# Score visits in pairs, with two score tiles and a third bank for the first matmul

## The chip, the cores and the metric

The kernel runs on one core of one Trainium2 chip. The metric is the device time of one execution in microseconds (us). The five engines of the core are TensorE (PE), VectorE (DVE), ScalarE (ACT), GpSimd (POOL) and SyncE (SP, which only issues DMAs here). PE writes its results into PSUM, which has eight banks of 512 fp32 columns on 128 partitions.

## The reference

Attention with a sliding window of 128 keys and a linear distance bias, in fp32, for 8 batches, 8 heads, 576 positions and head size 64; its output, as 4608 rows of 512, goes through a two-layer network of width 2048.

```python
scores = scale * np.matmul(q, k.transpose(0, 1, 3, 2))
bias = slopes[:, None, None] * (-np.abs(rel).astype(np.float32))[None, :, :]
mask = (rel >= 0) & (rel < window)            # window = 128
scores = np.where(mask, scores + bias[None], -1000000000.0)
attn = softmax(scores)                        # exp, row sums, division
x = np.matmul(attn, v) ...transposed to (4608, 512)
h = x @ w_in                                  # 512 -> 2048
g = h * (1.0 / (1.0 + np.exp(-beta * h)))
out = g @ w_out                               # 2048 -> 512
```

## The kernel before

All matmuls are bf16. The 4608 rows of x are taken in nine groups of 512 tokens (stage g). For each stage an **H step** `HS(g, j)` (j = 0 to 15, line 488) makes 128 of the 2048 columns with four matmuls of 512 columns into one PSUM bank; ACT then writes a tanh of it (`sig`, line 495) and DVE forms `gT` from `sig` and the bank (line 496). Only then is the bank free. **O steps** `OS(g, i, n)` (line 514) are quarters of an output tile, four matmuls each; after the fourth, the bank is copied to `osb` (DVE for g < 2, line 522, else ACT, line 524) and stored by DMA (for g < 2 from POOL's queue).

The attention of one batch runs ahead of the stages that need it. Batches 0 and 1 have functions of their own (`SP_`, `PVP`, `XP`, and for the last 64 rows `SCT`, `PV`, `X`). From batch 2 on:

- `get` loads q, k and v from SP's queue, `cast_qk` and `cast_v` turn them to bf16 on POOL, and `DT` transposes q and k by a DMA on SP's queue (line 382) into `QK[b % 2]`.
- A **score visit** `SC(b, m, p)` (line 404) makes, for the head pair p, the scores of key blocks 0 and 1 (m = 0) or 2 to 4 (m = 1). Head size is 64, so the two heads of a pair use 64 of the 128 rows each, side by side. All visits write the same two-bank tile `SS`. ACT takes the exp of its 1024 columns into `pt` (line 411), and DVE multiplies by a table of distances (`factor`, lines 158 and 163). There are 8 visits a batch, 48 in all.
- `PV(b, qb, g)` (lines 437 and 441) multiplies weights and values for four heads of a query block into a `pv` tile; column 64 is the row sum. `norm` divides on DVE (lines 327 and 328), and gives `xn`.
- `X(b, qb)` transposes `xn` into `XT`: for batches below 4 by PE and a DVE copy (lines 460 and 466), for the others by a DMA on SP's queue (line 455).

PSUM before: `SS` two banks; `psum_h` two banks (tag hps) for H; `psum_t` two banks (tag t) for `pv` and transposes; two banks that first hold `SX` of the opening and then, from `open_o` on, `psum_o` (tag ops) for O and, in stages 1 and 2, for odd H steps below 10 and 8.

The order on PE, SP and POOL is the order in which the program is written (`manual_schedule`); ACT and DVE are in written order in the opening alone, and a scheduler orders them later. The attention steps stand in a list `att` with weights. `merged` lays a half batch of visits beside the value steps of the half batch before (`pvx`), `jobs` are sprinkled in between, and `spread` hands steps out among the H and O steps of a stage in proportion to the weights, up to `need[g + 1]`, the last transposed result that the next stage reads:

```python
        for m in range(2):
            w = 5 if (b, m) == (2, 0) else 3
            a = [(None, lambda b=b, m=m, p=p: SC(b, m, p), w) for p in range(NP)]
            here += merged(a, before)
```

The opening (to about 50 us) is batches 0 and 1 with stage 0. On DVE, three copies `falls_rows` (line 140) for a table stand there ahead of the copy of `XP(0, 3)` into `XT` (line 355), and `falls_tail` (line 146) behind it.

Of the kernel before, what the change touches and what calls it, by code (L numbers as in the profile page):

```python
# [15 lines left out]
P = 128  # L16
# [3 lines left out]
def kernel(  # L20
# [62 lines left out]
    osb_pool = ctx.enter_context(tc.tile_pool(name="osb", bufs=4))  # L83
    psum_c = ctx.enter_context(tc.tile_pool(name="psum_c", bufs=1, space=bass.MemoryType.PSUM))
    psum_h = ctx.enter_context(tc.tile_pool(name="psum_h", bufs=2, space=bass.MemoryType.PSUM))
    psum_t = ctx.enter_context(tc.tile_pool(name="psum_t", bufs=2, space=bass.MemoryType.PSUM))
    SS = psum_c.tile([P, 2, 512], F32, name="SS")
    psum_c.seal()
    opening = ExitStack()
    psum_x = opening.enter_context(tc.tile_pool(name="psum_x", bufs=1, space=bass.MemoryType.PSUM))  # L90
    SX = psum_x.tile([P, 2, 512], F32, name="SX")
    late, gates = {}, {}

    def after(ins, other):
        tc.add_manual_dep(
# [149 lines left out]

    pts, xns = {}, {}

    def TP(b, p):
        src = staged.pop((b, "p", p))
        for i in (1, 0):  # L250
            tps = psum_t.tile([P, FULL], BF16, name="tps", tag="t")
            to = tps[:].rearrange("d (c r) -> d c r", c=4)
            if i == 0:
                to = tps[:].rearrange("d (k c r) -> d c k r", k=4, c=4)
            for c in range(4):
                nc.tensor.transpose(out=to[:, c], in_=src[:, i, c], identity=ident[:])
            if i:
                nc.vector.tensor_copy(
                    out=QK[b % 2][:, 1, p, 0:FULL].rearrange("d (r c) -> d r c", c=4),
                    in_=tps[:].rearrange("d (c r) -> d r c", c=4))  # L260
            else:
                nc.scalar.copy(out=QK[b % 2][:, 0, p, 0:FULL], in_=tps[:])
# [52 lines left out]
    def room(b, shape):  # L315

        if b == 0:
            return psum_h.tile(shape, F32, name="pvh", tag="hps")[:]
        if "o" in late:
            return late["o"].tile(shape, F32, name="pvo", tag="ops")[:]  # L320
        return psum_t.tile(shape, F32, name="pv", tag="t")[:]

    PLACES = {0: ((0, 0),), 1: ((0, 256), (1, 128)), 2: ((1, 256), (2, 0)), 3: ((2, 384), (3, 128))}
# [64 lines left out]

    COLS = {0: (0, 384), 1: (128, 256), 2: (0, 384), 3: (192, 320), 4: (128, None)}

    def SC(b, m, p):
        assert all((b, sb) in moved for sb in range((3, 5)[m]))
        qk = QK[b % 2]
        for kb in ((0, 1), (2, 4, 3))[m]:
            at, then = COLS[kb]
            nq = {3: P + 64, 4: 64}.get(kb, 2 * P)
            for e in range(2):
                o = SS[:, e, at : at + min(nq, 512 - at)]
                if kb in (0, 2):
                    o = bass.AP(  # L400
                        tensor=o.tensor, offset=o.offset,
                        ap=[list(o.ap[0]), [then - at, 2], [1, P]],
                    )
                nc.tensor.matmul(  # L404
                    o,
                    lhsT=qk[64 * e : 64 * e + 64, 1, p, P * kb : P * kb + P],
                    rhs=qk[64 * e : 64 * e + 64, 0, p, P * kb : P * kb + nq],
                    start=True, stop=True, skip_group_check=True,
                )
        pt = pt_pool.tile([P, 2, 512], BF16, name="pt", tag="pt")  # L410
        nc.scalar.activation(out=pt[:], in_=SS[:], func=ACTF.Exp, scale=qscale)  # L411
        factor(pt, m, p)
        pts[b, m, p] = pt

    def weights(b, kb, h, then):
        p, e = divmod(h, 2)
# [6 lines left out]
    def PV(b, qb, g):  # L423
        assert ("v", b, qb) in moved
        nq = ROWS[qb]
        vs = VS[b % 2]
        if g == 0:
            xns[b, qb] = xn_pool.tile([P, H, D], BF16, name="xn", tag="xn")
        xn = xns[b, qb]
        if b:  # L430
            pv = psum_t.tile([P, 4, 66], F32, name="pv", tag="t")
        else:
            pv = late["o"].tile([P, 4, 66], F32, name="pvo", tag="ops")
        for hl in range(4):
            h = 4 * g + hl
            if qb:
                nc.tensor.matmul(  # L437
                    pv[:, hl, 0 : D + 1], lhsT=weights(b, qb - 1, h, 1),
                    rhs=vs[:, qb - 1, h, 0 : D + 1], start=True, stop=False,
                )  # L440
            nc.tensor.matmul(  # L441
                pv[:, hl, 0 : D + 1], lhsT=weights(b, qb, h, 0),
                rhs=vs[:, qb, h, 0 : D + 1], start=qb == 0, stop=True,
            )
        norm(xn[0:nq, 4 * g : 4 * g + 4, :], pv, nq)

    def X(b, qb):
        nq = ROWS[qb]
        xnv = xns.pop((b, qb))[:].rearrange("p h d -> p (h d)")
        if b >= XDMA:  # L450
            tok0 = (b * S + P * qb) % XTR
            n1 = min(nq, XTR - tok0)
            for r0, r1, at in ((0, n1, tok0), (n1, nq, 0)):
                if r0 < r1:
                    nc.sync.dma_start(
                        out=XT[:, :, at : at + r1 - r0], in_=xnv[r0:r1], transpose=True)
            return
        xt = psum_t.tile([P, NDM, P], BF16, name="xt", tag="t")
        for c in range(NDM):
            nc.tensor.transpose(  # L460
                out=xt[:, c, 0:nq], in_=xnv[0:nq, c * P : (c + 1) * P],
                identity=ident[0:nq, 0:nq]
            )
        tok0 = (b * S + P * qb) % XTR
        n1 = min(nq, XTR - tok0)
        nc.vector.tensor_copy(out=XT[:, :, tok0 : tok0 + n1], in_=xt[:, :, 0:n1])
        if n1 < nq:
            nc.vector.tensor_copy(out=XT[:, :, 0 : nq - n1], in_=xt[:, :, n1:nq])
# [6 lines left out]
    def Hm(g, j, cs):  # L475
        if j == 0 and cs[0] == 0:
            gts[g] = gt_pool.tile([P, NFF, TOKG], BF16, name="gT", tag="gT")
        c0 = (g * TOKG) % XTR
        if cs[0] == 0:
            if g == 0 and j in (0, 3):  # L480
                hs[g, j] = SX[:, j // 2]
            elif j % 2 and j < FOUR.get(g, 0):
                hs[g, j] = late["o"].tile([P, DM], F32, name="hpo", tag="ops")[:]
            else:
                hs[g, j] = psum_h.tile([P, TOKG], F32, name="hps", tag="hps")[:]
        hps = hs[g, j]
        for c in cs:
            nc.tensor.matmul(  # L488
                hps, lhsT=W1[:, c, bass.ts(j, P)], rhs=XT[:, c, c0 : c0 + TOKG],
                start=(c == 0), stop=(c == NDM - 1),  # L490
            )
        if cs[-1] < NDM - 1:
            return
        sig = sig_pool.tile([P, TOKG], BF16, name="sig", tag="sig")
        gates[g, j] = nc.scalar.activation(out=sig[:], in_=hps, func=ACTF.Tanh, scale=beta_h[:, j : j + 1])  # L495
        gates["gT"] = nc.vector.scalar_tensor_tensor(  # L496
            out=gts[g][:, j, :], in0=sig[:], scalar=1.0, in1=hps, op0=ALU.add, op1=ALU.mult
        )
# [6 lines left out]
    def OS(g, i, n):  # L505
        gT = gts[g]
        if n == 0:
            late[g, i] = late["o"].tile([P, DM], F32, name="ops", tag="ops")
        ops_ = late[g, i][:]
        last = (g, i) == (NTG - 1, 3)  # L510
        for at in ((0, 256) if last else (0,)):
            cols = slice(at, at + 256) if last else slice(0, DM)
# [5 lines left out]
            if last or n == 3:  # L518
                osb = osb_pool.tile([P, DM], F32, name="osb", tag="osb")
                o = osb[:, 0 : cols.stop - cols.start]  # L520
                if g < 2 or at:
                    nc.vector.tensor_scalar_mul(o, ops_[:, cols], 0.5)  # L522
                else:
                    nc.scalar.mul(o, ops_[:, cols], 0.5)  # L524
# [22 lines left out]
    def pvx(b, qbs):  # L547
        r = []
        for qb in qbs:
            r += [(None, lambda g=g, qb=qb: PV(b, qb, g), 2) for g in range(2)]  # L550
            if b >= XDMA:
                r.append(((b, qb), lambda qb=qb: X(b, qb), 0))
            elif qb != qbs[0]:
# [17 lines left out]
    for b in range(2, B):  # L571
        here = []
        for m in range(2):
            w = 5 if (b, m) == (2, 0) else 3
            a = [(None, lambda b=b, m=m, p=p: SC(b, m, p), w) for p in range(NP)]
            here += merged(a, before)
            before = pvx(b, ((0, 1), (3, 4) if b < 4 else (2, 3, 4))[m])
        if b < 4:
# [1 line left out]
        if b + 1 < B:  # L580
            js, all_, n = jobs(b + 1), here, len(here)
            here = []
            for i, step in enumerate(all_):
                while js and js[0][0] * n <= 23 * i:
                    here.append((None, js.pop(0)[1], 0))
                here.append(step)
            here += [(None, j, 0) for _, j in js]
# [10 lines left out]
    with tc.manual_schedule(engines={ENG.PE, ENG.SP, ENG.Pool}):  # L598
        with tc.manual_schedule(engines={ENG.Activation, ENG.DVE}):
# [52 lines left out]
            PVP(0, "B", 3)  # L652
            XP(0, 1)
            XP(0, 2)
            for h in range(5, 8):
                falls_rows(h)
            Hm(0, 0, range(3))
            XP(0, 3)
            falls_tail()
            Hm(0, 1, range(3))  # L660
            for j in range(2):
                Hm(0, j, range(3, 4))
# [82 lines left out]
        def open_o():  # L745
            opening.close()
            late["o"] = ctx.enter_context(
                tc.tile_pool(name="psum_o", bufs=2, space=bass.MemoryType.PSUM))

        half = lambda c: lambda: Hm(0, 15, range(c, c + 2))  # L750
        steps = [h[2], R(0), h[3], A(0), h[4], R(1), B_(0), h[5], A(1), h[6], R(2), B_(1), VA(0),
                 h[7], A(2), R(3), h[8], VA(1), B_(2), VB(0), h[9], A(3), VB(1), VA(2), h[10],
                 B_(3), open_o, lambda: TT(0), h[11], VA(3), XO(0), lambda: SCT(0), h[12], VB(2),
                 XO(1), h[13], VB(3), lambda: PV(0, 4, 0), h[14], lambda: PV(0, 4, 1), XO(2),
# [1 line left out]
        for f in steps:  # L756
# [2 lines left out]
        h, o = HG(1), two(0) + OG(0, 2) + OG(0, 3) + two(1)  # L759
        o += OG(1, 2)  # L760
        rest = {0: [lambda: TT(1)], 2: [lambda: SCT(1)],
                4: [lambda: PV(1, 4, 0), lambda: PV(1, 4, 1)], 5: [lambda: X(1, 4)]}
        items = h[:10]
        for n in range(6):
            items += [h[10 + n], o[n]] + rest.get(n, [])
# [49 lines left out]
```

## Time and profile before

| | |
|---|---|
| median of 8 runs | 331.65 us (331.2 to 332.02) |
| the profiled execution | 331.98 us, its span 330.2 us |
| PE busy | 314.2 us, 95% of the span |
| DVE, ACT, POOL busy | 200.7, 186.6, 91.1 us |
| score visits, PE (line 404) | 240 matmuls, 18.9 us |
| exp of the visits (line 411) | 48 of 1019 ns |
| tanh and gT (lines 495, 496) | 688 and 683 ns each |
| DMA | 51.80 MB, mean 157 GB/s |

A row of the profile gives the line, the engine, the operation, the tiles as written<-read, the count, then busy time and mean duration, and the idle time of the engine just before, with what ended it. In a timeline the first number is the start in us from the span's start, the second the duration of the merged piece. The span is the time from the first to the last instruction; the execution's own time is 1.8 us longer.

### The profile page before, as it was taken

The page shows a single profiled execution, that of the slowest core. Times are in us where ns is not written, and L with a number is a line of the kernel's source. Part 1 is how long each engine was busy: PE and PEld are TensorE (multiplying, and loading weights), DVE is VectorE, ACT ScalarE, POOL GpSimd, SP SyncE. Part 2 cuts the span into 40 slices and gives each one's busy share as a digit, 9 for nine tenths or more (in the row PEclk, how much of TensorE's full clock was granted, in tenths as well). Part 3 has the DMA queues.
Part 4 walks back from the last instruction along what each step waited for, and adds up shares of the span by engine and source line. Part 5 has one row for each costly group of instructions (what it writes and reads, how often), then busy time and mean ns, then how long its engine had stood idle before and what let it go on. Part 6 is the DMA issues. An engine that isn't in the chain of part 4 may idle for free.

```text
span 330.2 us, 6005 instructions
## 1 busy us (share of the span) xinstructions
PE 314.2 (95%) x2252; PEld 150.7 (46%) x2294; DVE 200.7 (61%) x424; ACT 186.6 (56%) x265; POOL 91.1 (28%) x150
## 2 busy tenths in 40 slices
PE   7879979999999999999999999999999999999995
PEld 3444544443444454444444444344444445444443
DVE  6788777654859874866288627662877267334500
ACT  6849868614428744666476745664676465345511
POOL 4865611427445343432213222322000000000000
PEclk9999999999999999999999999999999999999999
DMA  7999999999999999997859896997022101210021
GB/s 218 254 256 249 182 198 215 204 193 238 217 217 239 191 209 267 195 188 163 193 121 215 180 217 129 203 186 158 18 64 57 64 16 50 58 63 33 5 93 64
DMA packets 147822, 51.80 MB, mean 157 GB/s; under 512 B 135360, under 2 KB 143824, under 8 KB 147792
## 3 DMA queue, kind: packets, MB, share of 16 engines
q1 hardware_dynamic: 139152, 38.29, 63.1%
q0 software_dynamic: 4864, 6.29, 9.8%
q10 hardware_dynamic: 3776, 6.83, 6.0%
q8 instruction: 18, 0.29, 0.4%
q14 instruction: 12, 0.10, 0.1%
HBM read 36.71 MB, written 9.44 MB: 140 GB/s over the span
## 4 chain that ended last, share of the span: by engine, by line
PE 85%; DVE 5%; ACT 4%; issue 2%; DMA 2%; SPq 1%; POOL 0%; ACTq 0%; DVEq 0%
PE ops L514 36%; PE hps L488 33%; PE SS L404 5%; PE hpo L488 2%; PE pv L441 2%; PE pv L437 2%; DMA fst<-in_q_dram 2%; DVE pt L163 1%; DVE gT L496 1%; ACT sig L495 1%; ACT pt L411 1%; PE xt L460 1%; SPq L205 1%; DVE fall L140 1%; ACT pt L311 1%
## 5 line engine op out<-in xcount | busy, mean ns | idle before, releaser
L514 PE MATMUL ops<-W,gT 128*128 128x512 bf16 (+1 forms) x574 | 136.1, 373 | 1.8 <-issue 0.6
L488 PE MATMUL hps<-XT,W 128*128 128x512 bf16 x511 | 131.5, 379 | 2.0 <-DVE gT L496 0.8
L496 DVE SCALAR_TENSOR_TENSOR gT<-sig,hps 128x512 bf16<-128x512 bf16 x133 | 90.3, 683 | 67.8 <-ACT sig L495 66.9
L495 ACT ACTIVATE sig<-hps,beta_h 128x512 bf16<-128x512 f32 x133 | 91.2, 688 | 60.9 <-PE hps L488 54.9
L514 PEld LDWEIGHTS <-gT 128*128 128x128 bf16 x592 | 54.1, 98 | 58.2 <-issue 3.0
L488 PEld LDWEIGHTS <-W 128*128 128x128 bf16 x576 | 50.6, 97 | 56.8 <-issue 6.9
L411 ACT ACTIVATE pt<-SS 128x1024 bf16<-128x1024 f32 x48 | 48.9, 1019 | 21.3 <-PE SS L404 21.3
L230 POOL CAST vs<-fst 128x512 bf16<-128x512 f32 (+1 forms) x40 | 26.6, 664 | 55.2 <-DMA fst<-in_v_dram 45.3
L524 ACT ACTIVATE osb<-ops 128x512 f32<-128x512 f32 (+1 forms) x28 | 16.5, 589 | 42.9 <-PE ops L514 42.9
L215 POOL CAST bst<-fst 128x512 bf16<-128x512 f32 (+1 forms) x32 | 20.6, 645 | 61.0 <-DMA fst<-in_q_dram 56.1
L328 DVE TENSOR_TENSOR xn<-pv,zs 128x256 bf16<-128x256 f32 (+1 forms) x62 | 26.0, 420 | 1.3
L163 DVE TENSOR_TENSOR pt<-pt,fall 128x1024 bf16<-128x1024 bf16 x24 | 20.2, 843 | 10.4 <-ACT pt L411 10.2
L216 POOL CAST bst<-fst 128x512 bf16<-128x512 f32 (+1 forms) x32 | 21.1, 660 | 16.1 <-DMA fst<-in_k_dram 16.0
L158 DVE TENSOR_TENSOR pt<-pt,falls 128x1024 bf16<-128x1024 bf16 x24 | 17.0, 709 | 12.0 <-ACT pt L411 11.9
L441 PE MATMUL pv<-vs,pt 128*128 128x65 bf16 x240 | 21.7, 193 | 0.1
L441 PEld LDWEIGHTS <-pt 128*128 128x128 bf16 x240 | 16.6, 97 | 8.6 <-DVE pt L163 0.2
L404 PE MATMUL SS<-qkT 64*128 64x256 bf16 (+2 forms) x240 | 18.9, 252 | 0.6
L437 PE MATMUL pv<-vs,pt 128*128 128x65 bf16 x192 | 18.1, 193 | 0.0
L437 PEld LDWEIGHTS <-pt 128*128 128x128 bf16 x192 | 15.2, 98 | 5.6
L522 DVE TENSOR_SCALAR osb<-ops 128x512 f32<-128x512 f32 (+1 forms) x9 | 5.9, 656 | 19.6 <-PE ops L514 19.6
L404 PEld LDWEIGHTS <-qkT 64*128 64x128 bf16 x240 | 8.0, 94 | 20.5 <-issue 19.5
L327 DVE RECIPROCAL zs<-pv 128x4 f32<-128x4 f32 (+1 forms) x67 | 11.1, 173 | 3.0 <-PE pv L441 2.1
(84 smaller groups left out, 182.0 us busy)
## 6 DMA issues: line engine op xcount, KB each, us to landing
fst<-in_k_dram SPq DMA_DIRECT2D x32, 256.0 KB, 5.5
fst<-in_q_dram SPq DMA_DIRECT2D x32, 256.0 KB, 5.5
fst<-in_v_dram SPq DMA_DIRECT2D x32, 256.0 KB, 4.4
out_dram<-osb ACTq DMA_DIRECT2D x26, 256.0 KB, 2.5
W<-in_moe_w_in_dram POOLq DMA_DIRECT2D x4, 512.0 KB, 8.1
W<-in_moe_w_out_dram POOLq DMA_DIRECT2D x4, 512.0 KB, 11.1
out_dram<-osb POOLq DMA_DIRECT2D x8, 256.0 KB, 4.3
fst<-in_q_dram SPq DMA_DIRECT2D x8, 128.0 KB, 3.7
```

The lines of the kernel that those rows point to most:

```text
L163: nc.vector.tensor_tensor(out=x, in0=x, in1=bass.AP(tensor=t.tensor, offset=t.offset, ap=[list(t.ap[0]), [P, 4], [0, 2], [1, P]]), op=ALU. ...
L216: return nc.gpsimd.tensor_copy(out=t[0:rows, 1], in_=fs.pop(("k", b, sb))[0:rows])
L230: return nc.gpsimd.tensor_copy(out=VS[b % 2][0:rows, sb, :, 0:D], in_=fs.pop(("v", b, sb))[0:rows])
L328: nc.vector.tensor_tensor(out=xn, in0=pv[0:nq, :, 0:D], in1=zs[0:nq].broadcast_to([nq, 4, D]), op=ALU.mult)
L404: nc.tensor.matmul(o, lhsT=qk[64 * e : 64 * e + 64, 1, p, P * kb : P * kb + P], rhs=qk[64 * e : 64 * e + 64, 0, p, P * kb : P * kb + nq], ...
L411: nc.scalar.activation(out=pt[:], in_=SS[:], func=ACTF.Exp, scale=qscale)
L437: nc.tensor.matmul(pv[:, hl, 0 : D + 1], lhsT=weights(b, qb - 1, h, 1), rhs=vs[:, qb - 1, h, 0 : D + 1], start=True, stop=False,)
L441: nc.tensor.matmul(pv[:, hl, 0 : D + 1], lhsT=weights(b, qb, h, 0), rhs=vs[:, qb, h, 0 : D + 1], start=qb == 0, stop=True,)
L488: nc.tensor.matmul(hps, lhsT=W1[:, c, bass.ts(j, P)], rhs=XT[:, c, c0 : c0 + TOKG], start=(c == 0), stop=(c == NDM - 1),)
L495: gates[g, j] = nc.scalar.activation(out=sig[:], in_=hps, func=ACTF.Tanh, scale=beta_h[:, j : j + 1])
L496: gates["gT"] = nc.vector.scalar_tensor_tensor(out=gts[g][:, j, :], in0=sig[:], scalar=1.0, in1=hps, op0=ALU.add, op1=ALU.mult)
L514: nc.tensor.matmul(ops_[:, cols], lhsT=gT[:, j, i * P : i * P + P], rhs=W2[:, j, cols], start=(j == 0), stop=(j == NFF - 1),)
```

## The change

Eight edits are made together.

1. `SC` takes two head pairs. The first visit writes `SS`, the second a new two-bank tile `ST`, with no other PE work between; two exps and two factors follow. The 48 visits become 24 pairs, each with twice the weight in `att`.
2. `ST` takes the banks of `psum_t`, which is closed by `open_s` in stage 1 (right behind `X(1, 4)`).
3. `PVB` replaces two `PV` from batch 2 on: all eight heads of a query block into a tile that `span()` gives, `SS` and `ST` in turn from `SS`, with one reciprocal and one multiplication. `X` for batches 2 and 3 writes its transposes, now plain matmuls with the identity, into the same tiles, and ACT copies them.
4. `psum_o` has one bank each for two tags, ops and h3. From stage 2 on, H steps with j % 3 == 2 use h3; odd steps below 10 in stage 1 and 8 in stage 2 take h3 or ops in turn. O(g, 0) uses an hps bank from stage 2 on, the other O steps ops.
5. The output copies of stages 0 and 1 go to ACT; only the last half tile stays on DVE.
6. No load, cast or q/k transpose is put directly ahead of a result transpose by DMA (batches 4 to 7).
7. In the opening, `XP(0, 3)` stands ahead of the three `falls_rows`, and `falls_tail` is written after `VA(0)` in the steps of stage 0. In the built program DVE runs the copy into `XT`, then the three `fall` copies, then the two of `falls_tail`, then the first `gT`.
8. `calm` puts two and one matmuls on zeros into an hps bank ahead of the two transposes of `TP(0, 1)`.

In the built program POOL's fourth store stands ahead of the first casts of batch 3, where it stood behind them.

```diff
+    spans = [SS]
+    def span():
+        spans.append(spans.pop(0))
+        return spans[-1]
+    def obank(name, tag=None):
+        if tag is None:
+            late["n"] = late.get("n", 0) + 1
+            tag = "ops" if late["n"] % 2 else "h3"
+        return late["o"].tile([P, DM], F32, name=name, tag=tag)[:]
...
+    def calm(n):
+        z = psum_h.tile([P, 512], F32, name="z", tag="hps")
+        for _ in range(n):
+            nc.tensor.matmul(
+                z[:], lhsT=zeros[:, 0:P], rhs=zeros[:], start=True, stop=True,
+                skip_group_check=True)
...
+            if (b, p) == (0, 1):
+                calm(1 + i)
...
-    def SC(b, m, p):
+    def SC(b, m, pp):
+        spans.sort(key=lambda t: t is not SS)
+        for p, sps in zip(pp, spans):
...
+        for p, sps in zip(pp, spans):
+            pt = pt_pool.tile([P, 2, 512], BF16, name="pt", tag="pt")
+            nc.scalar.activation(out=pt[:], in_=sps[:], func=ACTF.Exp, scale=qscale)
+            factor(pt, m, p)
+            pts[b, m, p] = pt
...
+    def PVB(b, qb):
+        pv = span()[:, :, 0 : 4 * 66].rearrange("p g (h x) -> p g h x", x=66)
+        for h in range(H):
...
+        nc.vector.reciprocal(out=zs[0:nq], in_=pv[0:nq, :, :, D : D + 1])
+        nc.vector.tensor_tensor(
+            out=xn[0:nq].rearrange("p (g h) d -> p g h d", g=2), in0=pv[0:nq, :, :, 0:D],
+            in1=zs[0:nq].broadcast_to([nq, 2, 4, D]), op=ALU.mult)
...
+        if b >= 2:
+            xt = span()[:, 0, :].rearrange("p (c q) -> p c q", c=NDM)
...
+            nc.scalar.copy(out=XT[:, :, tok0 : tok0 + n1], in_=xt[:, :, 0:n1])
...
             elif j % 2 and j < FOUR.get(g, 0):
-                hs[g, j] = late["o"].tile([P, DM], F32, name="hpo", tag="ops")[:]
+                hs[g, j] = obank("hpo", "h3" if j % 4 == 1 else "ops")
+            elif g > 1 and j % 3 == 2:
+                hs[g, j] = obank("hpo", "h3")
...
-            late[g, i] = late["o"].tile([P, DM], F32, name="ops", tag="ops")
+            if g < 2:
+                late[g, i] = obank("ops", "h3" if i % 2 and (g, i) != (1, 3) else "ops")
+            elif i == 0 or i == 2 and g == NTG - 1:
+                late[g, i] = psum_h.tile([P, DM], F32, name="oph", tag="hps")[:]
+            else:
+                late[g, i] = obank("ops", "ops")
...
-                if g < 2 or at:
+                if at:
...
-            r += [(None, lambda g=g, qb=qb: PV(b, qb, g), 2) for g in range(2)]
+            r.append((None, lambda qb=qb: PVB(b, qb), 4))
...
-            a = [(None, lambda b=b, m=m, p=p: SC(b, m, p), w) for p in range(NP)]
+            a = [(None, lambda b=b, m=m, p=p: SC(b, m, (p, p + 1)), 2 * w) for p in (0, 2)]
...
-                while js and js[0][0] * n <= 23 * i:
+                while js and js[0][0] * n <= 23 * i and (step[0] is None or b < XDMA):
...
             XP(0, 2)
+            Hm(0, 0, range(3))
+            XP(0, 3)
             for h in range(5, 8):
                 falls_rows(h)
-            Hm(0, 0, range(3))
-            XP(0, 3)
-            falls_tail()
...
+        def open_s():
+            trans.close()
+            psum_s = ctx.enter_context(
+                tc.tile_pool(name="psum_s", bufs=1, space=bass.MemoryType.PSUM))
+            spans.append(psum_s.tile([P, 2, 512], F32, name="ST"))
```

## The prediction

> **What bounds the kernel now.** I read, in this order: the page's busy rows and slices, the chain that ended last, the groups by line, TensorE's (PE's) timeline around one score visit, and the opening's timeline. A share of busy time alone says little, because ends of matmuls are modelled; so I also took start-to-start times from the trace.
>
> ```profile
> PE 314.2 (95%) x2252; PEld 150.7 (46%) x2294; DVE 200.7 (61%) x424; ACT 186.6 (56%) x265; POOL 91.1 (28%) x150
> ...
> PEclk9999999999999999999999999999999999999999
> DMA  7999999999999999997859896997022101210021
> ...
> PE 85%; DVE 5%; ACT 4%; issue 2%; DMA 2%; SPq 1%; POOL 0%; ACTq 0%; DVEq 0%
> ...
> L495 ACT ACTIVATE sig<-hps,beta_h 128x512 bf16<-128x512 f32 x133 | 91.2, 688 | 60.9 <-PE hps L488 54.9
> L411 ACT ACTIVATE pt<-SS 128x1024 bf16<-128x1024 f32 x48 | 48.9, 1019 | 21.3 <-PE SS L404 21.3
> ```
>
> PE carries 85% of the chain at full clock, ACT and DVE wait for it, and the DMA engines are over 90% busy in nearly every slice up to about 150 us. So PE time counts one for one, unless data arrive late. Where is PE time not spent on columns? Around a score visit (`SC`, rows of 64 instead of 128):
>
> ```profile
> 160.87 1.03 PE L488 MATMUL hps<-XT,W 128*128 128x512 bf16 x4
> ...
> 161.82 0.11 PEld L404 LDWEIGHTS <-qkT 64*128 64x128 bf16 x4 [0.42 <-issue]
> 161.83 0.39 PE L404 MATMUL SS<-qkT 64*128 64x256 bf16 x4
> ...
> 162.15 0.55 PEld L488 LDWEIGHTS <-W 128*128 128x128 bf16 x4 [0.21 <-issue]
> 162.15 1.04 PE L488 MATMUL hps<-XT,W 128*128 128x512 bf16 x4
> ...
> 163.03 0.81 PE L514 MATMUL ops<-W,gT 128*128 128x512 bf16 x3
> ```
>
> Start to start: the four H matmuls before the visit last 0.96 instead of the usual 0.86 us, the visit 0.325, the four behind it 0.873. One visit so costs 0.10 + 0.325 + 0.01 = 0.43 us. Inside visits of another form two row tiles of 64 columns, side by side, take 0.028 us, so 256 columns take 0.11 and a visit's 512 take 0.22. The other 0.21 is the change of row form, in and out; weights aren't loaded ahead across it (the idle times "issue" above). Over 48 visits that is some 10 us; all other PE waits behind 58 us are about 2.
>
> The opening has one large wait:
>
> ```profile
> 19.62 2.48 DVE L140 COPY fall<-fallq 128x256 bf16<-128x256 bf16 x3
> 22.02 0.68 DVE L355 CAST XT<-xtp 128x512 bf16<-128x512 f32 x1
> ...
> 20.84 0.81 PE L488 MATMUL hps<-XT,W 128*128 128x512 bf16 x3
> 22.75 0.38 PE L488 MATMUL SX<-XT,W 128*128 128x512 bf16 x1 [1.10 <-DVE XT L355]
> 26.42 0.34 PE L304 MATMUL SS<-qkT 64*128 64x256 bf16 x4 [0.45 <-ACT sig L495]
> ```
>
> PE stands because three table copies stand ahead of the XT copy on DVE; one of them took 1.90 us (the others 0.36 to 0.81) while POOL ran four casts from 19.05 to 21.58.
>
> **The change part by part**
>
> *Pairs (gain 5.0).* 48 visits become 24 pairs in SS and ST. A pair costs one visit more in columns, 0.43 + 0.22 = 0.65 us, against 2 x 0.43 = 0.86, so 0.21 each, 24 x 0.21 = 5.0. [...] The trace has both edges, 0.10 ahead of the visit and 0.11 in and behind it, so I take 5.0 [...].
>
> *Behind the pairs on ACT.* The two exps stand back to back: 2 x 1.02 = 2.04 us. Queued behind them are the tanh of H steps, and PE waits for the H bank until DVE's gT is through. [...] (a tanh at 151.52 follows the exp of 150.56 at once). Followed from H(j) that ends just as a pair begins: exps until +2.04, its tanh until 2.73, DVE's two factors (0.71 to 0.84 each) and its gT until about 3.5. With two H banks H(j+2) would come due 1.7 to 2.6 us later, so PE would wait 1 us or more per pair, and the 5 us would be gone several times over. The third bank makes H(j+3) the one that needs it: two H, an O quarter and mostly the pair or values lie between, 3.4 us or more. [...] with the third bank a wait of 0 to 0.2 us. I take 0.6 for all of stages 2 to 7, from 0 to 2.
>
> *PSUM otherwise.* ST takes psum_t's two banks, O keeps one bank (O(g,0) goes into an H bank). Between O(g,1) and O(g,2), and O(g,2) and O(g,3), stand two H steps, 1.73 us, against a copy of 0.60: hidden unless a pair of exps stands in front (2.6 in all; in the 0.6 above). PVB waits for the exp of its tile, and the next pair for PVB's norm; they lie 2.6 us and more apart, and one norm of 8 heads (0.18 + about 0.7, from 0.42 for 256 columns and 0.68 for 512) replaces two of 0.60. That takes some 10 us off DVE, which is not the bound: nothing.
>
> *Result transposes of batches 2, 3 and the first outputs to ACT.* Same matmul columns; ACT gets ten copies of up to 0.59 and eight of 0.60, about 10 us spread over 60 to 125 us, where it is busy under 60%. In the O-only stretch (75 to 96 us) today's PE waits are 1.1 us, the largest a transposition waiting for DVE:
>
> ```profile
> 94.44 0.28 PE L460 MATMUL xt<-ident,xn 128*128 128x128 bf16 x2 [0.48 <-DVE xn L328]
> ```
>
> With DVE relieved of the output copies and half of the norms I leave 0.4 of it: gain 0.7.
>
> *Opening (gain 0.8).* The XT copy can start when its matmuls are out (20.62 + 0.4 = 21.0) and ends at 21.7; PE goes on at 21.8, not 22.75. The three copies then run when POOL has ended its casts, so at 0.3 to 0.7 each, and falls_tail stays right behind them in DVE's order; the gT begin at about 23.0 instead of 23.88, the key copy for batch 1 ends 0.8 earlier, and with it the wait of 26.42. Bounds: if the copies take 0.8 each even now, the key copy comes 1.0 later and the gain becomes a loss of 1.0; I am near the uncontended rows since POOL has nothing from 21.58 to 24.55. The three idle matmuls of `calm` (3 x 0.22) lie in gaps of 0.33 and 0.47 before the second pair's transposes; they can push these by 0.1 to 0.4, but the third pair's start only at 9.76, when POOL has cast what the DMA brought: nothing. The clock row is at 9 in every slice, so they have no clock to win back.
>
> *Stage 2's start (loss 1.1).* Two things meet. H(2,1) and H(2,2) both get bank h3 (the odd-step rule gives it to 1, the by-three rule to 2), with only a pair (0.65) between; tanh and gT behind H(2,1) take 1.65. That is 1.0 of wait. And batch 3's first scores stand at 97.25, while their last transpose (issued 89.88, 5.8 us of latency) lands at 95.7. PE would now reach them at 97.25 - 0.8 - 1.5 = 95.0 plus. Also POOL's fourth output store now stands ahead of batch 3's first casts (79.76 before), and its value comes from ACT behind two exps, at about 81.2; SP's transposes stand behind those casts. So the landing can slip by up to 1.5. The two waits overlap; 1.0 to 2.0, I take 1.1.
>
> *SP's order.* For batches 4 to 7 each result transpose moves ahead of two or so loads. They land 2.4 us after issue (median), stage ends leave 6.9 us of O behind the last PVB, and loads lead by 7 us at batch 4: nothing; if a late norm held SP, loads behind it would slip by up to 1 us into that lead.
>
> **Sum** against the profiled execution (331.98, span 330.2): -5.0 - 0.7 - 0.8 + 1.1 + 0.6 = -4.8, so 327.2. That execution lies 0.33 above the median of the eight runs, so 326.9 as a median.
>
> **Rivals**
>
> *A, data-bound (0.20).* The DMA slices of 9 speak for it, the 7 us of lead from batch 4 on against it. What PE gains before batch 3's scores (0.8 + 0.7 + four pairs, 0.8 = 2.3) is then waited away, with 0.5 of slip on top, in place of the 1.1: -4.8 - 1.1 + 2.8 = -3.1, 328.6.
>
> *B, slower (0.13): ACT's bursts hold the H banks.* If the tanh behind a pair come so late that PE waits w per pair, the change loses once 24 w exceeds 4.8 + 0.6, w over 0.22 us. A DVE that is late by one more factor or norm (0.7 to 0.9) at half of the pairs gives w = 0.4: -5.4 + 9.6, 335.9. For it: ACT and DVE together serve every H step, and in stages 2 to 7 each is busy some 0.6 of the time in bursts. Against: today, with two banks and single exps, no such wait over 0.1 us shows.
>
> *C, the pairs don't save (0.07).* If ST isn't free when SS is, the second visit waits inside the pair, and the form changes are saved but the time isn't: with 0.12 per pair, -4.8 + 2.9, 330.
>
> **Numbers.** Forecast 0.60 for -4.8 with its own range 325.3 to 328.6. 0.2% is 0.66 us, about what a measurement of this kernel can tell from no change. Faster: 0.60 + 0.19 of A + 0.04 of C, with a little of B, 0.85; same 0.04; slower 0.11. The range of 8 in 10 goes from 325.0 (5.0, all 1.1 of the waits and 1.0 at the opening won, half a microsecond lost at stage 2) to 330.0 (A with 1.4 more of waits, and C).
>
> **What would show it.** Right: score pairs at 0.54 start to start with one 0.10 ahead; PE idle before L549 still near 2 us; the SX matmul at 21.8; the scores at 26.4 moved to 25.6. Wrong: PE waits of 0.2 and more on "DVE gT" or "ACT pt" behind pairs in every stage (B), PE waiting on the transposes of qkT around 95 us and again at batch 4 (A), or half pairs split by a wait (C).

## The result, and the profile after

| | before | after |
|---|---|---|
| median | 331.86 us (56 runs, 330.85 to 334.09) | 335.69 us (19 runs, 332.68 to 340.18) |
| ratio | | 1.0093, 95% interval 1.0076 to 1.0109 |
| the profiled execution's span | 330.2 us | 335.5 us (its time 337.25 us) |

The change makes the kernel 0.9% slower. Here and below, ratios leave out the most disturbed executions, so that a ratio can lie below the ratio of two medians. The profiled execution of after lies 1.6 us above its median; what follows is read from it. Its two largest waits recur in the experiments, at E3 for one with 3.2 and 2.3 us.

From the page of after, the rows that answer to those of before (busy time, clock, DMA share, the chain that ended last, then a tanh group and the two exp groups):

```profile
PE 312.9 (93%) x2254; PEld 153.8 (46%) x2297; DVE 186.7 (56%) x346; ACT 193.7 (58%) x283; POOL 88.7 (26%) x150
...
PEclk9999999999899999999999989999999999999999
DMA  7999999998999999997479990999320304210021
...
PE 75%; DMA 8%; DVE 5%; ACT 4%; SPq 4%; issue 2%; POOL 2%; DVEq 0%; ACTq 0%; POOLq 0%
...
L556 ACT ACTIVATE sig<-hps,beta_h 128x512 bf16<-128x512 f32 x99 | 68.0, 689 | 48.5 <-PE hps L549 44.8
...
L438 ACT ACTIVATE pt<-SS 128x1024 bf16<-128x1024 f32 x24 | 24.4, 1017 | 9.9 <-PE SS L430 9.9
...
L438 ACT ACTIVATE pt<-ST 128x1024 bf16<-128x1024 f32 x24 | 24.6, 1024 | 0.0
```

Three things are new. PE's share of the chain falls from 85% to 75%, and DMA with SP's queue rises from 3% to 12%. Two slices of the clock row show an 8. The DMA row has slices of 4 and 0 among the nines, where before had nothing under 5 up to the same place: in these slices the DMA engines are more than half idle, and in those behind them full.

The waits of PE in after (total, times, longest), with those of the opening left out:

```profile
PE hps L549 <- DMA XT<-xn: 4.4, 1, 4.4
PE hps L549 <- DMA qkT<-bst: 2.2, 1, 2.2
PE SS L430 <- DVE xn L492: 1.5, 1, 1.5
...
PE hpo L549 <- DVE gT L557: 1.0, 1, 1.0
...
PE ST L430 <- DVE xn L492: 0.4, 1, 0.4
```

The first two stand at the starts of stages 5 and 6: H(5,0) at 198.49 and H(6,0) at 233.84. The second is put down to a q/k transpose that landed at 233.33, but the result transpose that H(6,0) reads landed at 233.75, so it is the same wait as the first. Before, the last transposes landed at 193.49 and 226.60, and these H began at 194.32 and 226.93: 0.8 and 0.3 us to spare.

These waits are 9.5 us. Behind two of them the granted clock falls to one half (columns: window, length, busy time of PE, PEld, DVE, ACT and POOL, granted clock, DMA share, GB/s; each time the window ahead of the fall and the one behind it):

```profile
85.98:89.39 3.41, 1.51 (x16) 0.75 (x15) 2.64 (x6) 1.17 (x2) 0.36 (x1) 1.00 1.26 184
89.39:92.81 3.42, 3.42 (x16) 1.76 (x15) 1.37 (x2) 1.98 (x4) 1.93 (x4) 0.50 1.02 201
195.21:198.62 3.41, 0.13 (x1) 0.11 (x2) 0.00 (x0) 0.00 (x0) 0.72 (x2) 1.00 1.27 187
198.62:202.03 3.41, 3.41 (x9) 1.22 (x8) 0.69 (x1) 0.69 (x2) 1.29 (x3) 0.50 0.89 154
```

In these stretches matmuls of 512 columns stand 427 ns apart instead of 216. Half of 3.41 us is lost in each: 1.7 us. Waits and clock together are 12.9 us, and the span grew by 5.3; so the change won some 7.6 us, waits of before that are gone included, and lost more. The pairs themselves look as forecast:

```profile
177.19 1.03 PE L549 MATMUL hps<-XT,W 128*128 128x512 bf16 x4
178.14 0.40 PE L430 MATMUL SS<-qkT 64*128 64x256 bf16 x6
178.38 0.38 PE L430 MATMUL ST<-qkT 64*128 64x256 bf16 x6
178.69 1.04 PE L549 MATMUL hpo<-XT,W 128*128 128x512 bf16 x4
```

From 178.14 to 178.69 is 0.55 us for a pair, with 0.95 ahead of it for the four H matmuls (forecast: 0.54, and 0.10 more than the usual 0.86).

### The profile page after: what moved, and what is told of

Same layout as the page of the kernel before. It is cut to its first block, busy times and chain, and to the rows that moved or that the text cites. A ratio compares the mean times of both kernels' runs of the same rounds, so it can differ in the third digit from the quotient of the medians.

```text
span 335.5 us, 5971 instructions
## 1 busy us (share of the span) xinstructions
PE 312.9 (93%) x2254; PEld 153.8 (46%) x2297; DVE 186.7 (56%) x346; ACT 193.7 (58%) x283; POOL 88.7 (26%) x150
## 4 chain that ended last, share of the span: by engine, by line
PE 75%; DMA 8%; DVE 5%; ACT 4%; SPq 4%; issue 2%; POOL 2%; DVEq 0%; ACTq 0%; POOLq 0%
PE ops L580 24%; PE hps L549 23%; PE hpo L549 10%; PE oph L580 7%; DMA fst<-in_v_dram 3%; DMA fst<-in_q_dram 3%; ACT pt L438 2%; PE SS L430 2%; DVE pt L171 2%; SPq L218 2%; DMA XT<-xn 1%; PE SS L487 1%; PE ST L430 1%; SPq L207 1%; DMA qkT<-bst 1%
## 5 line engine op out<-in xcount | busy, mean ns | idle before, releaser
L580 PE MATMUL ops<-W,gT 128*128 128x512 bf16 (+1 forms) x450 | 109.2, 375 | 1.2 <-ACT osb L590 0.5
L557 DVE SCALAR_TENSOR_TENSOR gT<-sig,hps 128x512 bf16<-128x512 bf16 x99 | 67.3, 685 | 76.1 <-ACT sig L556 75.2
L549 PE MATMUL hps<-XT,W 128*128 128x512 bf16 x381 | 99.8, 384 | 7.4 <-DMA XT<-xn 4.4
L556 ACT ACTIVATE sig<-hps,beta_h 128x512 bf16<-128x512 f32 x99 | 68.0, 689 | 48.5 <-PE hps L549 44.8
L549 PE MATMUL hpo<-XT,W 128*128 128x512 bf16 x167 | 43.4, 379 | 1.2 <-DVE gT L557 1.0
L556 ACT ACTIVATE sig<-hpo,beta_h 128x512 bf16<-128x512 f32 x43 | 29.6, 689 | 15.6 <-PE hpo L549 13.3
L557 DVE SCALAR_TENSOR_TENSOR gT<-sig,hpo 128x512 bf16<-128x512 bf16 x43 | 29.4, 685 | 14.1 <-ACT sig L556 13.9
L438 ACT ACTIVATE pt<-SS 128x1024 bf16<-128x1024 f32 x24 | 24.4, 1017 | 9.9 <-PE SS L430 9.9
L580 PE MATMUL oph<-W,gT 128*128 128x512 bf16 x121 | 28.7, 379 | 0.3
L176 DVE TENSOR_TENSOR pt<-pt,fall 128x1024 bf16<-128x1024 bf16 x24 | 17.8, 747 | 13.0 <-ACT pt L438 12.9
L438 ACT ACTIVATE pt<-ST 128x1024 bf16<-128x1024 f32 x24 | 24.6, 1024 | 0.0
```

What stands on the lines that cost most here:

```text
L438: nc.scalar.activation(out=pt[:], in_=sps[:], func=ACTF.Exp, scale=qscale)
L549: nc.tensor.matmul(hps, lhsT=W1[:, c, bass.ts(j, P)], rhs=XT[:, c, c0 : c0 + TOKG], start=(c == 0), stop=(c == NDM - 1),)
L557: gates["gT"] = nc.vector.scalar_tensor_tensor(out=gts[g][:, j, :], in0=sig[:], scalar=1.0, in1=hps, op0=ALU.add, op1=ALU.mult)
L580: nc.tensor.matmul(ops_[:, cols], lhsT=gT[:, j, i * P : i * P + P], rhs=W2[:, j, cols], start=(j == 0), stop=(j == NFF - 1),)
```

## The experiments

Two theories at first: S, edit 6 (SP's order) makes the last result transposes late; P, the coarser steps (pairs, whole-block values) do so whatever stands on SP.

**E1, edit 6 undone.**

```diff
-                while js and js[0][0] * n <= 23 * i and (step[0] is None or b < XDMA):
+                while js and js[0][0] * n <= 23 * i:
```

> The changed kernel without edit 6: loads, casts and q/k transposes may again stand directly ahead of a result transpose on SP. Theory S (edit 6 is what makes the last result transposes of batches 5 and 6 land late): the waits of 4.6 us at H(5,0) and 2.4 us at H(6,0) go, and the half clock behind the first with them, so about 8 us less than the changed kernel, 327 to 329 us (ratio to the kernel before 0.985 to 0.992). Rival P (pairs and whole-block values are coarser steps, they push the jobs and the transposes together whatever stands directly ahead of them): H(5,0) and H(6,0) still wait 2 us or more each, 333 to 336 us.

Measured: 331.81 us (22 runs), ratio 1.0001 (0.9983 to 1.002). Its waits at the stage starts:

```profile
PE hps L549 <- DMA XT<-xn: 3.6, 2, 2.2
```

So edit 6 costs some 3.9 us in the median, half of what S claimed: 1.4 us stay at H(5,0) and 2.2 at H(6,0) (counted from start to start, as in the expectations below, 1.6 and 2.4). Neither theory is enough.

**E2, POOL's first stores between casts.** Around 86 us a score pair waits for the norm of a PVB, since PVB uses the score tiles. Ahead of that norm on DVE stands one factor, while POOL runs six casts on end (timelines of after, DVE, then POOL, then PE):

```profile
82.96 3.93 DVE L171 TENSOR_TENSOR pt<-pt,falls 128x1024 bf16<-128x1024 bf16 x1 [0.22 <-ACT pt L438]
86.81 0.19 DVE L491 RECIPROCAL zb<-SS 128x8 f32<-128x8 f32 x1
```
```profile
82.96 0.62 POOL L228 CAST bst<-fst 128x512 bf16<-128x512 f32 x1
...
85.74 0.60 POOL L229 CAST bst<-fst 128x512 bf16<-128x512 f32 x1
```
```profile
87.78 0.40 PE L430 MATMUL SS<-qkT 64*128 64x256 bf16 x6 [1.45 <-DVE xn L492]
88.62 0.40 PE L430 MATMUL ST<-qkT 64*128 64x256 bf16 x6 [0.44 <-DVE xn L492]
```

A factor takes 0.69 us in the median of after. The experiment puts the stores, which stood ahead of all six casts, between them:

```diff
         nc.gpsimd.tensor_copy(out=t[0:rows, 0], in_=fs.pop(("q", b, sb))[0:rows])
+        if b == 3 and waiting:
+            store()
...
-                if waiting:
+                if waiting and not (waiting[0][0] in (P, 2 * P, 3 * P) and (3, 3) not in moved):
```

> The changed kernel with POOL's first four output stores put between the first casts of batch 3, so that the casts begin about 2 us earlier and no six of them run back to back. Theory D (a DVE factor takes 3.93 us because POOL runs six casts on end, the norm behind it is late, and the next score pair waits for its tile): the factor falls to 2.5 us or less, the waits of 1.6 and 0.65 us ahead of and inside the pair at 86 to 88 us go, and no half clock follows; 2.5 to 3.8 us less than the changed kernel, 332 to 333 us. Rival A (the pair waits because two exps and two output copies stand on ACT): the wait stays at 1.5 us or more, time unchanged within 1 us of the changed kernel.

Measured: 335.02 us (13 runs), ratio 1.0076 (1.0046 to 1.0105). Locally D holds; two factors and the norm in E2:

```profile
82.22 2.12 DVE L171 TENSOR_TENSOR pt<-pt,falls 128x1024 bf16<-128x1024 bf16 x2 [0.47 <-ACT pt L440]
84.26 0.20 DVE L493 RECIPROCAL zb<-SS 128x8 f32<-128x8 f32 x1
```

Both PE waits are gone, no half clock follows there, and the seventeenth gT, which marks the start of stage 1, and the 33rd, that of stage 2, lie 44.8 us apart instead of 48.4. But H(5,0) and H(6,0) now wait 2.7 us each, with half clock behind both. In the median only 0.7 us is left of what was won ahead of stage 2, and these two waits are the likely reason. That was the hint: something other than PE sets when stages 5 and 6 may begin.

**E3, H(2,2) in an hps bank.**

```diff
-            elif g > 1 and j % 3 == 2:
+            elif g > 1 and j % 3 == 2 and (g, j) != (2, 2):
```

> The changed kernel with H(2,2) in an hps bank instead of h3, so that h3 is not used twice running at the start of stage 2. Theory: the wait of 1.17 us at 99.55 goes and nothing takes its place, 1.1 us less than the changed kernel. Rival: the scores of batch 3 next to it wait for their transposes instead (landed 97.4 and 100.1 us), and the time stays within 0.3 us of the changed kernel.

Measured: 333.96 us (17 runs), ratio 1.0052 (1.0031 to 1.0073). The wait on gT is gone; stage 2 takes 31.26 us instead of 31.76 from first gT to first gT, since a pair near 104.3 waits for its tile instead. Half of the wait is won; the rest of the gap in the medians isn't told apart from the clock.

**E4, single visits.**

```diff
-            a = [(None, lambda b=b, m=m, p=p: SC(b, m, (p, p + 1)), 2 * w) for p in (0, 2)]
+            a = [(None, lambda b=b, m=m, p=p: SC(b, m, (p,)), w) for p in range(NP)]
...
-        spans.sort(key=lambda t: t is not SS)
+        mine = [span() for _ in pp]
```

> The changed kernel with single score visits again, 48 of them, in SS and ST in turn; all other edits stay. If the pairs are worth what the prediction said (0.21 us each) and nothing else hangs on them, this is 5 us slower than the changed kernel, about 340 us. Rival P (the coarser steps make the transposes late): the waits at H(5,0) and H(6,0) fall by more than half and the time is below the changed kernel's, 331 to 334 us. Rival C (pairs save nothing): equal within 1 us, with the same waits.

Measured: 335.78 us (6 runs), ratio 1.0115 (1.008 to 1.015): as slow as after, and so between the expectations. The clock is full in its profile, and the waits at H(5,0) and H(6,0) are 1.1 and 1.7 us. Two things cancel. In stretches with eight visits and no large wait it takes 33.39 and 33.48 us where after takes 32.54 and 32.63, so a pair saves 0.21 us. Against that stand waits of 1.7 us on h3 and 1.5 on a norm, no smaller than after's. So finer steps lessen the waits at the stage starts: P is true in part. E4 undoes the pairs alone; what the whole-block values add was not measured by themselves.

**E5 and E7, v loads on another queue.** E5 is E1 with the v loads of batches 5 to 7 issued by POOL; E7 is E5 with the edits of E2 and E3.

```diff
-        return nc.sync.dma_start(
+        queue = nc.gpsimd if what == "v" and b > XDMA else nc.sync
+        return queue.dma_start(
```

> The changed kernel without edit 6 (as in the first experiment, 331.8 us), and with the v loads of batches 5 to 7 issued from POOL's queue instead of SP's. Theory Q (what is left of the waits at H(5,0), 1.6 us, and H(6,0), 2.4 us, is SP's queue: v loads and q/k transposes that wait for POOL's casts stand ahead of the last result transposes): the last result transposes are issued 1.5 to 3 us earlier, both waits fall below 0.6 us, 328 to 329.5 us. Rival L (the landing is late because the DMA engines are full and the values late, not the queue): the waits stay above 1 us each, within 1 us of 331.8.

> The changed kernel without edit 6, with H(2,2) in an hps bank, POOL's first stores between the casts of batch 3, and the v loads of batches 5 to 7 on POOL's queue. If the four losses are separate and nothing else comes due, they add up: 331.8 less 1.1 (h3), less 1.8 (pair at 86 us), less 3.5 (stage starts) gives 325 to 326 us. If the stage starts are bound by the stream of loads (rival L), what is won before them is waited away there: 329 to 331 us.

Measured: E5 334.67 us (12 runs, 329.4 to 343.21), ratio 0.9961 (0.9934 to 0.9989); E7 331.8 us (14 runs, 325.96 to 340.69), ratio 0.9887 (0.9849 to 0.9925). Times now scatter by 14 us: five of E5's twelve executions took 329.4 to 331.2 us, the profiled one 340.66. That one waits 3.5 us at H(5,0) and 6.0 at H(6,0). Q is not borne out, and the four repairs of E7 don't add up in the median: with five loads fewer on SP for a batch, E7's last result transposes left SP 1.2 and 0.6 us behind their norms (2.3 and 3.5 in E1), but then took 5.8 us to land (4.15 in E1), and so landed within 0.6 us of E1's. One q/k transpose in E7 took 10.4 us from issue (172.08) to landing (182.46). Why loads from two queues scatter so is open.

**E6, edit 6 alone in the kernel before.** The edit is the line of E1, the other way.

> The kernel before with edit 6 alone, nothing else changed. In the kernel before the last result transposes land only 0.8 and 0.3 us ahead of H(5,0) and H(6,0). If edit 6 alone makes SP late, H(5,0) and H(6,0) wait 1 to 3 us each and it is 2 to 5 us slower than before, 334 to 336 us. If edit 6 hurts only together with the coarser steps, it is within 0.7 us of the kernel before.

Measured: 331.89 us (22 runs), ratio 0.9997 (0.9985 to 1.0008). Edit 6 hurts only together with the coarser steps. In the issue order of SP the reason can be seen. Before and after, ahead of the first result transpose of batch 4:

```profile
155.73 0.58 SPq L194 DMA_DIRECT2D fst<-in_q_dram  x1
156.37 0.58 SPq L194 DMA_DIRECT2D fst<-in_k_dram  x1
156.99 0.92 SPq L194 DMA_DIRECT2D fst<-in_q_dram  x1
157.96 1.23 SPq L194 DMA_DIRECT2D fst<-in_k_dram  x1
166.97 1.21 SPq L455 DMA_TRANSPOSE XT<-xn  x1
```
```profile
157.88 0.58 SPq L207 DMA_DIRECT2D fst<-in_q_dram  x1
158.51 0.57 SPq L207 DMA_DIRECT2D fst<-in_k_dram  x1
168.69 1.21 SPq L504 DMA_TRANSPOSE XT<-xn  x1
```

SP stands at that transpose for 8 to 10 us, until the norm has come, and all loads written behind it stand too. Before, four loads went out first; after, two. With `n` at 14 steps instead of 23, the second pair of loads comes due just at the step of the transpose, where edit 6 holds it back.

**E8, idle matmuls inside the waits.**

```diff
     def HS(g, j):
+        if j == 0 and g in (5, 6):
+            calm((12, 6)[g - 5])
```

> The changed kernel with 12 idle matmuls on zeros (2.6 us of PE time) written ahead of H(5,0) and 6 (1.3 us) ahead of H(6,0), inside the waits of 4.6 and 2.4 us. Theory K (a long wait costs twice, since TensorE runs at half clock for about 3 us behind it): no half clock behind H(5,0) and H(6,0), the waits for data end at the same time, and the median falls by 1.7 to 3 us, to 333 to 334 us; single times spread less. Rival: the clock falls whatever PE does in the wait, and the time is the changed kernel's, 335 to 336 us, or more by what the idle matmuls overrun.

Measured: 333.87 us (16 runs), ratio 1.0057 (1.0031 to 1.0083): 1.8 us below after with more work on PE. The mean granted clock is 1.0 to within 0.002 in 11 of 16 executions (332.5 to 334.6 us), where after has it in 2 of 20 (one more is on record with its clock than the 19 of the table): in after two executions at 1.0 took 332.2 and 332.7, eight at about 0.995 took 334.2 to 335.6, seven at 0.99 took 335.7 to 339.3, and three at 0.985 took 338.1 to 340.2. K holds in the median: filling the waits took half clock away in most executions. It did not in all; in E8's profile one wait was still long enough:

```profile
191.84 2.75 PE L265 MATMUL z<-zeros 128*128 128x512 bf16 x12
197.05 3.36 PE L549 MATMUL hps<-XT,W 128*128 128x512 bf16 x8 [2.45 <-DMA XT<-xn]
...
229.80 1.46 PE L265 MATMUL z<-zeros 128*128 128x512 bf16 x6
232.19 1.89 PE L549 MATMUL hps<-XT,W 128*128 128x512 bf16 x8 [0.93 <-DMA XT<-xn]
```

Eight matmuls take 3.36 us behind the gap of 2.45, and 1.89 behind that of 0.93.

**E9, eight loads ahead of the standing transpose.** Theory B came from E2, E5 and E6: the DMA engines are partly idle while SP stands, and full from then until the last transposes land. E9 is E1 with:

```diff
-            r.append((2 * sb, lambda sb=sb: (get("q", b, sb), get("k", b, sb))))
+            r.append((0 if b > XDMA and sb < 4 else 2 * sb, lambda sb=sb: (get("q", b, sb), get("k", b, sb))))
```

> The changed kernel without edit 6, and with eight q/k loads of the next batch (batches 5 to 7) written ahead of the first result transpose of the batch before, instead of four. Theory B (SP stands for 5 to 10 us at the first result transpose of a batch while the DMA engines are idle; from its norm to the last transpose's landing the DMA engines are then full for 26.5 us; edit 6 left two loads ahead of that point instead of four and made it 29.8 us): the stretch from the first transpose's issue to the landing of the last falls from 26.8 to 22 to 24 us, the waits at H(5,0) (1.6 us) and H(6,0) (2.4 us) go, 327 to 329 us. Rival L (the landing is set by the values, not by the loads behind the standing transpose): the waits stay above 1 us, 331 to 332 us.

Measured: 326.83 us (6 runs, 326.71 to 327.13), ratio 0.9832 (0.9793 to 0.9871). The windows ahead of and behind the first result transpose of batch 4, in before, after and E9 (second number from the right: DMA share):

```profile
158.00:167.00 9.00, 8.95 (x61) 4.01 (x60) 3.73 (x8) 4.37 (x8) 2.45 (x4) 1.00 0.69 161
167.00:194.00 27.00, 26.57 (x190) 12.60 (x193) 17.46 (x36) 16.52 (x22) 7.71 (x11) 1.00 1.02 188
```
```profile
159.00:168.00 9.00, 8.95 (x61) 4.24 (x60) 4.08 (x8) 5.03 (x7) 1.22 (x2) 1.00 0.44 118
168.00:199.00 31.00, 26.28 (x190) 12.84 (x193) 16.33 (x28) 15.45 (x22) 8.24 (x13) 0.99 1.08 192
```
```profile
158.00:167.00 9.00, 8.95 (x62) 4.28 (x61) 4.56 (x8) 5.04 (x7) 2.46 (x4) 1.00 1.05 242
167.00:194.00 27.00, 26.69 (x194) 13.20 (x197) 15.61 (x27) 15.78 (x23) 6.75 (x11) 1.00 0.96 184
```

The same nine microseconds ahead of the transpose carry 161, 118 and 242 GB/s; behind it all three are near the same rate, at a full share. What isn't loaded while SP stands comes later, ahead of the last transposes. From the first transpose's issue to the landing of the one that H(5,0) needs are 26.5 us before, 29.8 after, 26.8 in E1 and 22.8 in E9, where it lands at 190.04 and PE comes to it at 192.42. At H(6,0) nothing is to spare even in E9: landed 223.66, begun 223.70. PE's waits at the stage starts are gone; the longest of E9 behind the opening are the two of stages 1 and 2:

```profile
PE SS L430 <- DVE xn L492: 1.0, 1, 1.0
PE hpo L549 <- DVE gT L557: 1.0, 1, 1.0
```

**E10, E9 with the edits of E2 and E3.**

> The last one with H(2,2) in an hps bank and POOL's first stores between the casts of batch 3. If the stage starts no longer wait for data, the 1.1 and 1.8 us won before them now count: 324.5 to 326.5 us. If the data of stages 5 and 6 still bound it, the two repairs are waited away there and it is within 1 us of the last one.

Measured: 326.34 us (6 runs, 324.59 to 327.8), ratio 0.9811 (0.9767 to 0.9855), the lowest median here, but only 0.5 us under E9's (1.2 in the profiled spans), which six runs of each don't tell apart. Stages 5 and 6 don't wait; batch 3's first scores do:

```profile
PE SS L432 <- DMA qkT<-bst: 1.3, 1, 1.3
```

**E11, edit 6 with the eight loads**, that is, after with E9's line. ("The first one" in its text is E9.)

> The changed kernel, edit 6 included, with the eight loads written ahead of the first result transpose as in the first one of this call. Theory B: edit 6 cost time only because it pushed two loads behind the transpose at which SP stands; with eight ahead it costs nothing, and the time is that of the first one of this call within 1 us. Rival (edit 6 costs time through the order of later transposes and loads): 2 us or more above it.

Measured: 328.9 us (6 runs, 325.52 to 330.7), ratio 0.9871 (0.9821 to 0.9921). The place of the loads gives back nearly 7 us, but 2.1 us over E9 stay, and 2.0 us of wait at H(6,0). So edit 6 costs by the later order on SP too: H(6,0)'s transpose is issued at 221.25, in E9 at 219.38, though its norm is done at the same time (217.97 and 218.13).

**E12, the eight loads in the kernel before.**

> The kernel before with the eight loads ahead, nothing else. There PE, not the data, ends last (the last transposes land 0.8 and 0.3 us before they are needed), so Theory B expects no change beyond 0.5 us, 331.4 to 332 us, though the last transposes land some 2 to 4 us earlier. If the kernel before already lost time to the same standing queue, it is faster by 1 us or more.

Measured: 331.76 us (22 runs), ratio 0.9988 (0.9972 to 1.0004). As B expects: the transposes land 3.5 and 2.6 us earlier (190.02 and 223.97), and where PE ends last, that brings nothing that can be told from no change.

## Why the prediction was wrong

- **SP's order: the step that failed.** It was costed at nothing, with a landing time of 2.4 us (the median), 6.9 us of O matmuls behind the last PVB and 7 us of lead for loads at batch 4. What it left out is how long a result transpose, its values ready, still stands on SP behind what was put there earlier. For H(5,0), in after and then in before: the last norm, and SP from there to the transpose with its values, which is the row of two pieces (x2; in after the row at 191.01 is of the block before it):

```profile
188.32 0.69 DVE L492 TENSOR_TENSOR xn<-SS,zb 128x512 bf16<-128x512 f32 x1
189.58 1.32 SPq L405 DMA_TRANSPOSE qkT<-bst  x1
191.01 1.21 SPq L504 DMA_TRANSPOSE XT<-xn  x1
192.27 1.59 SPq L207 DMA_DIRECT2D fst<-in_v_dram  x2
193.96 2.52 SPq L504 DMA_TRANSPOSE XT<-xn  x2
```
```profile
187.44 0.42 DVE L328 TENSOR_TENSOR xn<-pv,zs 128x256 bf16<-128x256 f32 x1
189.56 2.84 SPq L455 DMA_TRANSPOSE XT<-xn  x2
```

| us from norm to issue, from issue to landing | before | after | E1 | E9 |
|---|---|---|---|---|
| for H(5,0) | 1.7, 3.9 | 4.9, 4.5 | 2.3, 4.15 | 0.0, 2.3 |
| for H(6,0) | 2.1, 3.9 | 4.7, 3.2 | 3.5, 4.15 | 1.25, 4.3 |

So the queue is the larger part of what after lost. By estimate from these times, a transpose issued at once and as slow as after's would have landed at 193.5, while PE had work until 194.07. In front of it stood q/k transposes, which waited for POOL's casts (3.5 us between 186 and 196 us), as POOL waited for loads. The landing time was wrong as well: of before's twelve transposes that landed in under 2.5 us, eight stand behind 230 us, where the DMA row shows 2 and less. And the lead at batch 4 says nothing of the result transposes, which had 0.8 and 0.3 us to spare before. With so little, the 4.8 us that PE was to win could not count ahead of stage 6 unless the transposes moved too. They went the other way: 6.6 us of waits, and 1.7 of half clock.

- **Rival A** (data-bound) had the right resource at the wrong place, batch 3, with a cost of 2.8. Its "7 us of lead" was the same misreading.
- **Pairs, 5.0: right.** Before took 33.53 and 33.27 us for two stretches with eight visits, after 32.54 and 32.63: 1.63 over eight pairs, 0.20 each; E4 gives 0.21.
- **Behind the pairs on ACT, 0.6: less.** No wait on a tanh or gT stands behind pairs, apart from the 1.0 us with h3.
- **Stage 2's start, 1.1: right in size,** 1.0 on gT. Batch 3's transposes were no wait in after, and became one where work ahead of them was quicker (E7 1.1 us, E10 1.3) or SP's order was changed (E11 0.4).
- **"PSUM otherwise", nothing, and the O-only stretch, gain 0.7: wrong.** The cover, "2.6 us and more" between PVB's norm and the next pair, was gone once POOL's casts, kept back behind a fourth store, ran in one burst beside a factor. Waits there came to 1.9 us in after, with 1.7 of half clock behind them (1.4 and none in E1 and E9). Before's trace already showed a table copy of 1.90 us beside four casts, and that was used for the opening alone. A factor took 3.93 us beside six casts on end of 0.60 to 0.62 us each, 1.06 beside casts that alternate with stores (E2: 2.12 for two), and 0.69 in the median of after. The long one began with the first cast, at 82.96, and ended 0.55 us behind the last. The runs show that the two go together, not how the casts hold a factor up.
- **Opening, 0.8: the matmul and the scores as said** (21.85 and 25.65), but by the first O matmul only part is left: 59.2 us in before and E12, 58.8 on average in after, E1 to E4 and E9 to E11: 0.4, with single traces between 58.5 and 59.3. **calm, nothing:** three waits for POOL's casts, 1.0 us in all (1.2 before).

E9 keeps every edit but 6, and loads in time: 4.9 us under the kernel before, where the sum said 4.8. That it fits so well is partly chance. With the pairs (4.9) and the opening (0.4) as measured, and the 2.4 us of waits that stages 1 and 2 still have, the sum gives 2.9, an estimate from these traces; the other 2.0 were won where no run here separates the edits.

## What to carry to other kernels

Before a gain on the bounding engine is counted, look up at each stage start how long ahead the last input had landed: that slack (0.8 and 0.3 us in before), not the mean load of the DMA, is the most that can be won there, unless the input moves forward too. Ask also when its values were ready: the time from there to the issue (for H(5,0) 1.7 us in before, 4.9 in after) went to what stood ahead of it in the queue. On SP's queue a result transpose that waited 8 to 10 us for its norm held back every load written behind it; what counted was how many loads stood ahead of it (four in before, two in after, eight in E9: 161, 118 and 242 GB/s meanwhile), and a finer or coarser step list changes that without a line about loads. A wait of PE can cost half clock on top: in after, 1.7 us each behind the waits of 4.4 us and of 1.9 (1.5 and 0.4), none behind that of 2.2.

## What the runs showed of the hardware

The half clock was not in the prediction. The stretches at half clock behind these waits last 3.41 us, and within one execution all changes of the clock lie whole multiples of 3.41 us apart (after: 89.39, 92.81, 198.62, 202.03; E2: 194.72, 198.13, 228.85, 232.26). These points cut a trace into windows of 3.41 us. PE was not idle throughout the windows that ended in a fall: past the opening, the clock fell at the end of windows that still held 1.51 us (after), 1.36 (E8), 1.27 and 1.10 (E2) of PE work. It didn't fall at the end of windows with 1.69 (E4) and 1.80 us (E1), nor behind one with 1.47 (E7). So the border lies near 1.5 us of work in these traces, not sharply, and the length of a wait alone doesn't decide: the 2.45 us of E8 lay mostly in one window, the 3.0 of E7 (191.60 to 194.60) was split by a border at 192.66, and the waits of 2.2 us at H(6,0) in after and E1 left 2.29 and 1.80 us of work in the window. This goes some way to explain why executions of one kernel differ: after's spread over 8 us, from 332.2 at clock 1.0 to 340.2 at 0.984.
